# Gated attention, a token mixer and two feed-forward blocks on one core: scores of two block rows in one PSUM pass, full-height blocks in the token mixing, two more heads turned on TensorE

## The chip, the core and the metric

One core of a Trainium2 chip runs one program. Its engines are TensorE (PE, whose weight loads are shown as PEld), VectorE (DVE), ScalarE (ACT), GpSimd (POOL) and SyncE (SP, which here issues every DMA). Each engine works through its own list in order; semaphores join the lists. The metric is the device time of one launch in microseconds, the median of several runs.

## The reference, cut to what matters

```python
# 4 batches x 8 heads, 576 positions, 64 per head: 32 heads in all
scores = (q @ k.T) / 8 + (cum[i] - cum[j])       # cum = cumsum(log f); above the diagonal -1e9
attn = softmax(scores); x = attn @ v             # per head
# token mixing (over the 576 positions), per batch, then channel mixing
h = relu(x.T @ w_tok1) @ w_tok2                  # 576 -> 256 -> 576
u = x + h.T
x2 = u + relu(u @ w_ch1) @ w_ch2                 # 512 -> 1536 -> 512
# second block: 512 -> 1024, a 3-tap convolution over positions as a gate, -> 512
hh = relu(x2 @ w_in); out = (hh * sigmoid(conv(hh))) @ w_out
```

The weights arrive as 64-bit floats and are decoded on the chip.

## The kernel before, in words

**Precision by splitting.** Most products are made from a high and a low part of each operand: `mm3` (lines 231 to 236) issues three matmuls, high by high (L234), high by low (L235), low by high (L236). High parts are written by ACT, low parts by DVE or POOL.

**Attention.** Heads run in pairs. The 576 query rows of a head are cut into five block rows i = 0 to 4 of 64, 128, 128, 128, 128 rows; for causality block row i needs `W[i]` = 64, 192, 320, 448, 576 key columns. `score(p, i)` (lines 666 to 693) makes one block row for both heads of a pair: two matmuls of q by k (L688, one head in array rows 0 to 63, the other in rows 64 to 127) and two that add the decay (`dec`, a row vector spread by `sel`, L692), into a PSUM tile "z". There are two z tiles of two banks each; block row 4 takes both, one a head; any other takes one for both heads. `smax` (L706, DVE) adds the mask and takes the row maximum, `sexp` (L712, ACT) the exponential, into an SBUF tile `t`. A z tile is free again when DVE has read it for both heads.

**Turning the probabilities.** The product with v needs `t` transposed. For heads with `BY_PE` (0 to 7, 30, 31) TensorE turns 13 blocks of 128x128 a head (`ptr`, L745). Heads 0 to 7 are copied out in fp32 (L223, L758); heads 30 and 31 are split into two fp16 halves, the high one by ACT (L763), the low one by DVE (L766). For heads 8 to 29 POOL writes the high half (`hi_part`, L721), DVE the low half (`lo_part`, L727), and two DMA transposes (L737) turn them. Then come the product with v (`pv`, L777 or L782 to L784), and `norm` and `xout` (L789 to L801) on DVE, the split of x by ACT (`xh`) and POOL (`xl`).

**Token mixing.** Four heads make a group, two groups a batch. `t1(g, a)` multiplies x by `w_tok1` over the positions: five blocks, of which block 0 has 64 rows and is contracted with a 64-row matmul, the others 128. `t2(g, d, e)` first turns x into PSUM (`t2_x`, L921: three transposes, of which one is a 64-row or a 32-row one), then adds the second product. From its PSUM tile ACT writes the high part `uh` and a copy `us`; the low part `ul` is written by DVE from PSUM for groups in `SOON` (0, 1, 7), by POOL from the copy for the others.

**Channel mixing and the second block.** Once a batch's u is there, `channel_mix` over the first three of twelve weight blocks is put in as filler between the attention's work; the rest runs after the attention, then the second block. These are long rows of 128x288 matmuls.

**What sets the order.** `Order` collects every task with an engine, a duration, a rank and its dependences, plans them (of the tasks that an engine can start earliest, the lowest rank first; buffers such as the two z tiles and four one-bank "w" tiles count), and then emits the instructions in the planned order. `PER`, the planned time of a head, enters the ranks. The plan is fixed when the program is built: what stands at the head of an engine's list and has to wait holds up all behind it.

Of the kernel before, what the change touches and what calls it, by code (L numbers as in the profile page):

```python
# [9 lines left out]
F32R = mybir.dt.float32r  # L10
# [137 lines left out]
def fox_moe_kernel(  # L148
# [54 lines left out]
    BY_PE = [n < 8 or n >= NH - 2 for n in range(NH)]  # L203

    FULL = 2 * HG
    PER = 7.0
# [12 lines left out]
    def f32(ap):  # L219
        return ap.bitcast(F32)  # L220
# [257 lines left out]
    with tc.manual_schedule():  # L478
# [11 lines left out]
        dec = ap1.tile([128, QKW - S], F32R, name="dec", bufs=1)  # L490
# [39 lines left out]
        nc.scalar.activation(out=dec[:, 0:S], in_=cum, func=AF.Copy, scale=-8.0)  # L530
        for a in (1, 3):
            r = slice(NH * a, NH * a + NH)
            nc.vector.scalar_tensor_tensor(dec[r, 0:S], cum[r], -8.0, f32(dec[r, 0:S]), ALU.mult, ALU.subtract)
        nc.scalar.activation(out=dec[:, S:QKW - S], in_=f32(dec[:, 0:QKW - 2 * S]), func=AF.Copy)
# [59 lines left out]
        def v_pow(g):  # L594
            sc = ap1.tile([128, 2], F32, tag="vsc", name="vsc", bufs=3)
            nc.vector.tensor_scalar(sc[:, 0:1], vps_t[g], 2.0 ** -86, None, ALU.max)
            si = sc[:, 0:1].bitcast(I32)
            nc.vector.tensor_scalar(si, si, 0x7F800000, 0x7F800000, ALU.bitwise_xor, ALU.bitwise_and)
            nc.vector.tensor_scalar(sc[:, 0:1], sc[:, 0:1], 8192.0, None, ALU.mult)
            nc.vector.tensor_scalar(sc[:, 1:2], sc[:, 0:1], PSC * 1e-9, None, ALU.mult)  # L600
            vs_t[g] = sc
# [44 lines left out]
        w1l = ap1.tile([128, NS, TOK], F32R, tag="w1l", name="w1l", bufs=1)  # L646
        w2h = ap1.tile([128, KT, S], F32R, tag="w2h", name="w2h", bufs=1)
# [20 lines left out]
        def score(p, i):  # L668
            t = qk_t[p % QKB]
            w = W[i]  # L670
            rows = 64 if i == 0 else 128
            if i == 4:
                z = [bank("z") for _ in range(2)]
                hw = w // 2
                spans = [(S + 64 + e * hw, hw) for e in range(2)]
                out_ = [[z[x][:, e, 0:hw] for e in range(2)] for x in range(2)]
                for x in range(2):
                    z_t[2 * p + x, i] = z[x][:, :, 0:hw]
            else:
                z = bank("z")  # L680
                spans = [(S, w)]
                out_ = [[z[0:rows, x, 0:w]] for x in range(2)]
                for x in range(2):
                    z_t[2 * p + x, i] = z[0:rows, x, 0:w]
            halves = [slice(64 * x, 64 * x + 64) for x in range(2)]
            for e, (k0, n) in enumerate(spans):
                for x, r in enumerate(halves):
                    nc.tensor.matmul(out_[x][e], t[r, Q0[i]:Q0[i] + rows], t[r, k0:k0 + n], start=True, stop=False)  # L688
            for e, (k0, n) in enumerate(spans):
                for x, r in enumerate(halves):  # L690
                    h = 2 * p + x
                    nc.tensor.matmul(out_[x][e], sel[r, h:h + 1].to_broadcast([64, rows]), dec[r, k0 - S:k0 - S + n],  # L692
                                     start=False, stop=True)
# [127 lines left out]
        PE_S = {4: 1.42, 3: 1.16, 2: 0.89, 1: 0.61, 0: 0.44}  # L821
# [4 lines left out]
        def pair(p):  # L826
# [5 lines left out]
            for i in ORDER:  # L832
                kz = [turn("z") for _ in range(2 if i == 4 else 1)]
                T("PE", PE_S[i], t0 + 1, score, p, i, reads=[kq], writes=[*kz, ("scores",)], pools=A2 + A1, ring=kz)
                for x in range(2):
                    n = 2 * p + x
                    kt = ("t", n % TB)
                    rank = t0 + x * PER
                    T("DVE", DVE_S[i], rank + 2, smax, n, i, reads=[kz[x % len(kz)]], writes=[(*kt, i), ("m", n % 3, i)],
                      pools=A2 + A1, ring=[kz[x % len(kz)]])  # L840
                    T("ACT", ACT_E[i], rank + 3, sexp, n, i, reads=[("m", n % 3, i)], writes=[(*kt, i)], pools=A2)
# [42 lines left out]
        def t1(g, a):  # L884
# [4 lines left out]
            for j in range(NS):  # L889
                r = slice(0, 64 if j == 0 else 128)  # L890
                terms.append((w1h[r, j, c], w1l[r, j, c], st["xh"][r, j, :], st["xl"][r, j, :]))
# [14 lines left out]

        SEGS = [[], []]
        for j in range(NS):
            s0, n = (0, 64) if j == 0 else (64 + 128 * (j - 1), 128)
            for e in range(2):  # L910
                lo, hi = max(s0, e * CH), min(s0 + n, e * CH + CH)
                if lo < hi:
                    SEGS[e].append((j, n, lo - s0, hi - s0, lo - e * CH, hi - e * CH))

        def t2_x(g, d, e):

            st = tok[g]
            ps = bank("w")[:, 0:CH]
            c = slice(d * 128, (d + 1) * 128)
            for k, (j, n, a0, a1, b0, b1) in enumerate(SEGS[e]):  # L920
                nc.tensor.matmul(ps[:, b0:b1], xf_t[g][a0:a1, j, c], ident[a0:a1, a0:a1], is_transpose=True, start=(k == 0),  # L921
                                 stop=False)
            st["ps2", d, e] = ps
# [34 lines left out]
        SOON = (0, 1, NG - 1)  # L958
# [259 lines left out]
```

## Time and profile before

| | us |
|---|---|
| median of 3 runs | 781.96 |
| lowest, highest | 779.5, 787.52 |
| the profiled execution | 782.84 |
| its span, first to last instruction | 781.0 |
| TensorE busy | 762.8 (98%) |
| VectorE busy | 491.5 (63%) |
| GpSimd busy | 364.7 (47%) |
| ScalarE busy | 338.7 (43%) |

Attention, token mixing and the filler take the first 290 us; the rest is channel mixing and the second block. A busy time counts an instruction from its start to its modelled end; matmuls overlap, so what a matmul costs TensorE is read from one start to the next, not from its duration. A pair's start is below that of its first score matmul with 288 columns (block row 4): pair 4 (heads 8 and 9) starts at 76.85 us, pair 5 at 107.12, pair 11 (heads 22 and 23) at 198.31.

### The profile page before, as it was taken

Reading aid. Unit: us, or ns where it says so; the run is one execution under the profiler, and the core shown is the slowest. Engines: PE = TensorE matmul, PEld = TensorE weight load, DVE = VectorE, ACT = ScalarE, POOL = GpSimd, SP = SyncE. Lnnn points to the kernel's source line nnn. Section 1 sums busy time; section 2 is a strip of 40 time slices with the busy share of each in tenths; the row PEclk is TensorE's granted clock in tenths of the full one; section 3 lists DMA queues with packets and bytes.
Section 4 is the critical chain, followed back from the end, with each engine's and each line's share of the span. In section 5 each row is a group of like instructions: output and inputs, shape, how many; then the busy total and the mean of one; then the engine's idle time right before and its main releaser. Section 6 shows DMA issues by size and latency. Waiting matters only on the chain.

```text
span 781.0 us, 16260 instructions
## 1 busy us (share of the span) xinstructions
PE 762.8 (98%) x6428; PEld 714.1 (91%) x6428; DVE 491.5 (63%) x1075; ACT 338.7 (43%) x753; POOL 364.7 (47%) x448
## 2 busy tenths in 40 slices
PE   7999899999999999999999999999998999999997
PEld 5888788888888899999999999999998999999997
DVE  5687869777695667688731221124799866787651
ACT  5676545566465555653320220122453333233321
POOL 3253635784757335454521221223666655565441
PEclk6899889999999999999999999999999999999999
DMA  9344489899997906755442122124421110100000
GB/s 222 102 159 151 153 168 194 170 220 204 199 183 156 188 2 213 266 192 162 129 138 75 39 70 84 31 69 146 161 77 47 53 55 31 54 20 20 31 33 31
DMA packets 133453, 91.69 MB, mean 117 GB/s; under 512 B 86848, under 2 KB 125504, under 8 KB 133376
## 3 DMA queue, kind: packets, MB, share of 16 engines
q1 hardware_dynamic: 133376, 90.65, 45.1%
q8 instruction: 50, 0.82, 0.4%
q14 instruction: 27, 0.22, 0.1%
HBM read 53.01 MB, written 18.87 MB: 92 GB/s over the span
## 4 chain that ended last, share of the span: by engine, by line
PE 84%; DVE 10%; DMA 2%; ACT 1%; issue 1%; POOL 1%; SPq 0%; POOLq 0%; ACTq 0%; DVEq 0%
PE w L234 14%; PE w L235 13%; PE w L236 13%; PE z L235 8%; PE z L234 8%; PE z L236 8%; PE z L688 7%; PE w L777 3%; DVE cv L1119 3%; PE w L921 2%; PE z L692 2%; PE w L745 2%; DVE wexp L307 1%; PE w L782 1%; PE w L783 1%; PE w L784 1%
## 5 line engine op out<-in xcount | busy, mean ns | idle before, releaser
L234 PE MATMUL w<-uh,ww2a 128*128 128x288 f32 x352 | 104.3, 296 | 0.6 <-DVE r L425 0.5
L235 PE MATMUL w<-ul,ww2a 128*128 128x288 f32 x352 | 103.8, 295 | 0.0
L236 PE MATMUL w<-uh,ww2a 128*128 128x288 f32 x352 | 103.6, 294 | 0.0
L421 ACT ACTIVATE r<-w 128x288 fp32r<-128x288 f32 x96 | 39.0, 408 | 132.0 <-PE w L236 131.2
L712 ACT ACTIVATE t<-t,m 128x320 f32<-128x320 f32 (+4 forms) x160 | 82.5, 554 | 30.0 <-DVE m L706 27.1
L1119 DVE SCALAR_TENSOR_TENSOR cv<-hp,cw,cv 128x286 f32<-128x286 f32 (+1 forms) x128 | 89.1, 696 | 4.5
L234 PE MATMUL w<-uh,ww 128*128 128x288 f32 x288 | 86.8, 301 | 0.5 <-ACT hp L1112 0.5
L425 DVE SCALAR_TENSOR_TENSOR r<-w,r 128x288 fp32r<-128x288 f32 x96 | 42.9, 454 | 70.3 <-ACT r L421 70.0
L234 PE MATMUL z<-r,ww2b 128*128 128x288 f32 x288 | 85.0, 295 | 0.0
L235 PE MATMUL w<-ul,ww 128*128 128x288 f32 x288 | 85.0, 295 | 0.0
L706 DVE CUSTOM_DVE_ANT_0 t<-z,mask 128x320 f32<-128x320 f32 (+4 forms) x160 | 71.6, 482 | 21.3 <-PE z L692 20.6
L235 PE MATMUL z<-r,ww2b 128*128 128x288 f32 x288 | 84.8, 295 | 0.0
L236 PE MATMUL w<-uh,ww 128*128 128x288 f32 x288 | 84.7, 294 | 0.0
L236 PE MATMUL z<-r,ww2b 128*128 128x288 f32 x288 | 84.7, 294 | 0.0
L229 POOL TENSOR_TENSOR ul<-u,uh 128x288 fp32r<-128x288 f32 x64 | 57.9, 930 | 54.5 <-ACT uh L223 54.5
L234 PE MATMUL z<-g,ww2a 128*128 128x286 f32 (+1 forms) x256 | 76.1, 297 | 2.2 <-ACT o L223 1.0
L235 PE MATMUL z<-g,ww2a 128*128 128x286 f32 (+1 forms) x256 | 76.3, 298 | 1.6 <-POOL g L229 1.6
L236 PE MATMUL z<-g,ww2a 128*128 128x286 f32 (+1 forms) x256 | 75.4, 295 | 0.0
L688 PE MATMUL z<-qk 64*128 64x288 f32 (+4 forms) x384 | 67.6, 441 | 7.8 <-DVE m L706 5.6
L442 POOL TENSOR_TENSOR res<-res,u 128x288 f32<-128x288 f32 x32 | 26.2, 820 | 93.1 <-DVE res L439 85.9
L234 PEld LDWEIGHTS w<-uh,ww2a 128*128 128x128 f32 x352 | 66.0, 187 | 1.0 <-DVE r L425 1.0
L236 PEld LDWEIGHTS w<-uh,ww2a 128*128 128x128 f32 x352 | 66.3, 188 | 0.0
(136 smaller groups left out, 2187.4 us busy)
## 6 DMA issues: line engine op xcount, KB each, us to landing
wraw<-in_moe_w_ch_dram SPq DMA_DIRECT2D x24, 512.0 KB, 4.0
qk<-in_qk_dram SPq DMA_DIRECT2D x16, 608.0 KB, 4.4
u_d<-us SPq DMA_DIRECT2D x8, 576.0 KB, 4.4
p_d<-res SPq DMA_DIRECT2D x32, 144.0 KB, 3.1
u<-u_d SPq DMA_DIRECT2D x8, 576.0 KB, 5.0
res<-p_d SPq DMA_DIRECT2D x32, 144.0 KB, 2.6
x_d<-res SPq DMA_DIRECT2D x32, 144.0 KB, 1.8
u<-x_d SPq DMA_DIRECT2D x8, 576.0 KB, 4.1
```

The source lines that it names most:

```text
L229: nc.gpsimd.tensor_tensor(o, a, b, ALU.subtract)
L234: nc.tensor.matmul(ps, wh, xh, start=(first and i == 0), stop=False)
L235: nc.tensor.matmul(ps, wh, xl, start=False, stop=False)
L236: nc.tensor.matmul(ps, wl, xh, start=False, stop=(last and i == n - 1))
L421: nc.scalar.activation(out=t[:, 0, :], in_=box["z", m], func=AF.Relu)
L425: nc.vector.scalar_tensor_tensor(t[:, 1, :], box["z", m], 0.0, f32(t[:, 0, :]), ALU.max, ALU.subtract)
L442: nc.gpsimd.tensor_tensor(box["res", d], box["res", d], ubox["u"][:, d], ALU.add)
L688: nc.tensor.matmul(out_[x][e], t[r, Q0[i]:Q0[i] + rows], t[r, k0:k0 + n], start=True, stop=False)
L706: nc.vector.tensor_tensor_reduce(to, z_t.pop((n, i)), mk, -0.125, 3e38, ALU.add, ALU.min, m_t[n][0:rows, i:i + 1])
L712: nc.scalar.activation(out=tt[0:rows, o:o + w], in_=tt[0:rows, o:o + w], func=AF.Exp, bias=m_t[n][0:rows, i:i + 1], scale=-1.0)
L777: nc.tensor.matmul(o[:, 0:65], p32(n)[:, 128 * blk:128 * blk + 128], vp32_t[g][:, slot, hh, :], start=(j == 0), stop=(j == nb - 1))
L1119: nc.vector.scalar_tensor_tensor(cv, hp[:, s0 + t:s1 + t], cw[:, t, m:m + 1], cv, ALU.mult, ALU.add)
```

## The change

Block rows 0 and 3 now share one z bank a head (64 + 448 = 512 columns), and so do 1 and 2 (192 + 320); the decay of both is added by one matmul of 512 columns, for which `dec` holds the needed pieces side by side. A 64-row block 0 is made with all 128 rows (the lower 64 are not read). In `t1` block 0 is contracted over 128 rows, the lower 64 of its weights being zero; in `t2_x` the transposes that straddle a chunk are made whole, and only the 64-row one is left. Heads 8 and 9 are turned by TensorE. The low part of u of groups 2 and 3 (the second batch) is written by DVE. `PER` goes from 7 to 6, and the planner's score durations follow the new blocks.

```diff
-    BY_PE = [n < 8 or n >= NH - 2 for n in range(NH)]
+    BY_PE = [n < 10 or n >= NH - 2 for n in range(NH)]
-    PER = 7.0
+    PER = 6.0
...
+        DEC4, DEC12 = 128, S + 128
+        dec = ap1.tile([128, DEC12 + 512], F32R, name="dec", bufs=1)
+        dmain = dec[:, 64:64 + S]
...
-        nc.scalar.activation(out=dec[:, S:QKW - S], in_=f32(dec[:, 0:QKW - 2 * S]), func=AF.Copy)
+        for a, n in ((DEC12 - 64, 64), (0, 64), (DEC12, W[1]), (DEC12 + W[1], W[2])):
+            nc.scalar.activation(out=dec[:, a:a + n], in_=f32(dmain[:, 0:n]), func=AF.Copy)
...
+        nc.gpsimd.memset(f32(w1h[64:128, 0]), 0.0)
+        nc.gpsimd.memset(f32(w1l[64:128, 0]), 0.0)
...
+        SETS = {(4,): DEC4, (0, 3): 0, (1, 2): DEC12}
-        def score(p, i):
+        def score(p, blocks):
...
+                z = bank("z")
+                sums = [([z[:, x, :] for x in range(2)], d0, 512)]
+                products = []
+                at = 0
+                for i in blocks:
+                    products.append((i, [z[:, x, at:at + W[i]] for x in range(2)], S, W[i], at == 0))
...
+            for i, out_, k0, n, first in products:
                 for x, r in enumerate(halves):
-                    nc.tensor.matmul(out_[x][e], t[r, Q0[i]:Q0[i] + rows], t[r, k0:k0 + n], start=True, stop=False)
+                    nc.tensor.matmul(out_[x], t[r, Q0[i]:Q0[i] + 128], t[r, k0:k0 + n], start=first, stop=False)
...
-        PE_S = {4: 1.42, 3: 1.16, 2: 0.89, 1: 0.61, 0: 0.44}
+        PE_S = {(4,): 1.42, (0, 3): 1.33, (1, 2): 1.28}
...
-                r = slice(0, 64 if j == 0 else 128)
-                terms.append((w1h[r, j, c], w1l[r, j, c], st["xh"][r, j, :], st["xl"][r, j, :]))
+                terms.append((w1h[:, j, c], w1l[:, j, c], st["xh"][:, j, :], st["xl"][:, j, :]))
...
-            for k, (j, n, a0, a1, b0, b1) in enumerate(SEGS[e]):
-                nc.tensor.matmul(ps[:, b0:b1], xf_t[g][a0:a1, j, c], ident[a0:a1, a0:a1], is_transpose=True, start=(k == 0),
-                                 stop=False)
+            for k, (j, b) in enumerate(SEGS[e]):
+                n = 64 if j == 0 else 128
+                nc.tensor.matmul(ps[:, m + b:m + b + n], xf_t[g][0:n, j, c], ident[0:n, 0:n], is_transpose=True,
+                                 start=(k == 0), stop=False)
...
-        SOON = (0, 1, NG - 1)
+        SOON = (0, 1, 2, 3, NG - 1)
```

The order is planned anew. TensorE's list before, from the product with v of heads 6 and 7 (`vp`, `pt`) to the token mixing of group 1 (`xh`, `w1h`); between them stand block rows 3, 2, 1, 0 of pair 4:

```order
L777 MATMUL w<-vp_149,pt 128x65 x30
L688 MATMUL z<-qk_105 128x448 x2
L692 MATMUL z<-dec,sel 128x448 x2
L688 MATMUL z<-qk_105 128x320 x2
L692 MATMUL z<-dec,sel 128x320 x2
L688 MATMUL z<-qk_105 128x192 x2
L692 MATMUL z<-dec,sel 128x192 x2
L688 MATMUL z<-qk_105 64x64 x2
```

The same place in the changed program (`ident,t` are the transposes of heads 8 and 9, the 288-column scores are block row 4 of pair 5):

```order
L704 MATMUL z<-dec,sel 128x512 x2
L789 MATMUL w<-vp_152,pt 128x65 x15
L700 MATMUL z<-qk_105 128x192 x2
L700 MATMUL z<-qk_105 128x320 x2
L704 MATMUL z<-dec,sel 128x512 x2
L757 MATMUL w<-ident,t_139 128x128 x8
L757 MATMUL w<-ident,t_140 128x128 x8
L595 MATMUL w<-vacc,ones 128x1
L700 MATMUL z<-qk_106 128x288 x4
L704 MATMUL z<-dec,sel 128x288 x4
L234 MATMUL w<-xh,w1h 128x256
```

The scores now stand on both sides of head 7's product with v, and 16 transposes and pair 5's first scores stand between that product and the token mixing of its group.

VectorE's list before at this place: `rs` and `xf` are norm and xout of heads 6 and 7, the `wexp` triples decode weights, the last row reads the first score tile of block row 3:

```order
L801 TENSOR_TENSOR xf<-w,rs 128x5x64
L305 TENSOR_SCALAR wexp<-wexp 128x512
L306 SCALAR_TENSOR_TENSOR wexp<-wraw,wexp 128x512
L307 SCALAR_TENSOR_TENSOR wexp<-wraw,wexp 128x512
L789 TENSOR_SCALAR rs<-w 128x5
L793 RECIPROCAL rs<-rs 128x5
L305 TENSOR_SCALAR wexp<-wexp 128x512
L306 SCALAR_TENSOR_TENSOR wexp<-wraw,wexp 128x512
L307 SCALAR_TENSOR_TENSOR wexp<-wraw,wexp 128x512
L801 TENSOR_TENSOR xf<-w,rs 128x5x64
L706 ISA t_136,m<-z,mask 128x448
```

And in the changed program, from the norm of head 6 to the xout of head 7:

```order
L805 RECIPROCAL rs<-rs 128x5
L718 ISA t_139,m<-z,mask 128x448
L718 ISA m 128x1
L813 TENSOR_TENSOR xf<-w,rs 128x5x64
L718 ISA t_139,m<-z,mask 64x64
L718 ISA m 64x1
L718 ISA t_140,m<-z,mask 128x448
L718 ISA m 128x1
L801 TENSOR_SCALAR rs<-w 128x5
L805 RECIPROCAL rs<-rs 128x5
L718 ISA t_140,m<-z,mask 64x64
L718 ISA m 64x1
```

No weight is decoded between the two heads any more; the two decodes stand ahead of head 6's norm instead.

## Rows read from the trace of the kernel before

**Rows 1.** The page: busy time, share, instructions; TensorE's clock in 40 slices.

```profile
PE   762.8 (98%) x6428; PEld 714.1 (91%) x6428; DVE 491.5 (63%) x1075; ACT 338.7 (43%) x753; POOL 364.7 (47%) x448
```

**Rows 2.** Busy time by stretch, then granted clock, DMA share, GB/s.

```profile
76.85:107.12 30.27, 26.89 (x177) 23.22 (x177) 23.00 (x52) 15.89 (x35) 16.54 (x19) 0.83 0.54 145
107.12:198.31 91.19, 90.26 (x1036) 75.72 (x1035) 69.44 (x200) 55.02 (x119) 53.78 (x53) 1.00 0.95 196
...
120.00:140.00 20.00, 19.14 (x226) 15.99 (x222) 17.79 (x53) 11.96 (x24) 11.19 (x13) 1.00 1.13 203
```

**Rows 3.** TensorE's timeline at pair 4: start, us, line, idle before and its releaser.

```profile
88.02 0.55 PE L692 MATMUL z<-dec,sel 64*128 64x320 f32 x2
91.07 0.60 PE L688 MATMUL z<-qk 64*128 64x192 f32 x4 [2.50 <-DVE m L706]
...
92.03 0.36 PE L234 MATMUL w<-xh,w1h 64*128 64x256 f32 x1
93.27 0.58 PE L235 MATMUL w<-xl,w1h 64*128 64x256 f32 x1 [0.89 <-POOL xl L229]
```

**Rows 4.** TensorE's timeline: scores that stand alone, then two block rows in one run.

```profile
169.07 1.02 PE L688 MATMUL z<-qk 64*128 64x448 f32 x4
...
170.22 0.40 PE L234 MATMUL w<-r,ww 128*128 128x288 f32 x1
...
170.82 0.81 PE L688 MATMUL z<-qk 64*128 64x320 f32 x4
...
171.71 0.40 PE L234 MATMUL w<-r,ww 128*128 128x288 f32 x1
...
189.06 1.02 PE L688 MATMUL z<-qk 64*128 64x448 f32 x4
...
190.90 0.40 PE L234 MATMUL w<-uh,ww 128*128 128x288 f32 x1
```

**Rows 5.** The same view: block rows 1 and 0 in one run.

```profile
146.21 0.59 PE L688 MATMUL z<-qk 64*128 64x192 f32 x4
...
147.26 0.40 PE L234 MATMUL w<-uh,ww 128*128 128x288 f32 x1
```

**Rows 6.** The same view: token mixing across its 64-row block.

```profile
142.43 0.28 PE L236 MATMUL w<-xh,w1l 128*128 128x256 f32 x1
142.64 0.38 PE L234 MATMUL w<-xh,w1h 64*128 64x256 f32 x1
...
143.41 0.28 PE L235 MATMUL w<-xl,w1h 128*128 128x256 f32 x1
143.53 0.28 PE L236 MATMUL w<-xh,w1l 128*128 128x256 f32 x1
```

**Rows 7.** The same view: `t2_x` with its 32-row transpose; 16 transposes of `ptr`.

```profile
105.56 0.29 PE L236 MATMUL w<-w2h,t1l 128*128 128x288 f32 x1
105.78 0.62 PE L921 MATMUL w<-ident,xf 32*128 32x32 f32 x3
106.15 0.38 PE L234 MATMUL w<-w2h,t1h 128*128 128x288 f32 x1
...
35.19 1.97 PE L745 MATMUL w<-ident,t 128*128 128x128 f32 x16
```

**Rows 8.** VectorE by line and shape, 57.84 to 260.85 us: count | busy us, mean ns.

```profile
L727 DVE SCALAR_TENSOR_TENSOR pl<-t,ph 128x1024 f16<-128x1024 f32 x21 | 28.8, 1373 | 1.2 <-POOL ph L721 1.0
L727 DVE SCALAR_TENSOR_TENSOR pl<-t,ph 128x640 f16<-128x640 f32 x21 | 23.3, 1115 | 4.9 <-POOL ph L721 4.9
...
L948 DVE TENSOR_TENSOR ul<-w,uh 128x288 fp32r<-128x288 f32 x8 | 3.7, 456 | 3.9 <-ACT us L223 3.8
```

**Rows 9.** The same view, 270 to 290 us: the low half of heads 30 and 31.

```profile
L766 DVE SCALAR_TENSOR_TENSOR pt<-w,pt 128x512 f16<-128x512 f32 x6 | 3.9, 685 | 0.1
```

## What the change will do to the time: the prediction

> **What bounds the kernel now.** I read the page's busy times first, then busy time by stretch, then TensorE's timeline at single places, then VectorE by line and shape. The page has TensorE busy 98% of the span [rows 1]; no other engine is near. That share is counted to modelled ends, so I took what a matmul costs from the distance between starts: two 256-column matmuls in a row start 0.12 us apart (143.41 to 143.53 [rows 6]), so by columns 288 take 0.135. From 290 us on the program is almost nothing but rows of 288, and the change does not touch them. So what it can change lies in the first 290 us, where TensorE pays for its own work and for what it waits for.
>
> The largest wait is at pair 4. The score matmuls that start at 88.02 are followed by the next at 91.07, where TensorE waited 2.50 us for VectorE to empty a z tile; at 92.03 one matmul of the token mixing starts and its neighbour only at 93.27, after 0.89 us for GpSimd's `xl` [rows 3]. Against the usual spacing these are 2.6 and 1.0 us. And the clock falls: over the 30.27 us from pair 4 to pair 5 the granted clock is 0.83 [rows 2], which with the two levels of 1.2 and 2.4 GHz is a third of the stretch, 10.3 us, at the lower one. Work of about 5 us took 10. The whole place costs 2.6 + 1.0 + 5 = 8.6 us. What came before the fall were these two waits; in the 20 us of [rows 2] with the clock at 1.00 TensorE was kept busy.
>
> **The change, part by part.** *Scores.* Block row 3 alone takes 170.22 - 169.07 = 1.15 us for 448 columns, block row 2 takes 171.71 - 170.82 = 0.89 for 320; both in one run take 190.90 - 189.06 = 1.84 [rows 4]. So a run has a fixed part of about 0.20 us, and the rest goes by columns. A run also costs its neighbours: the three 288-column matmuls between two runs, 170.22 to 170.82, take 0.60 us where 3 x 0.135 is 0.40. That makes 0.40 us a run. The column total of a pair is the same before and now (1600 a head). What goes is runs: in the two lists of TensorE I counted 58 and 38 runs of scores, 20 x 0.40 = 8.0 us. Block row 0 also no longer changes the array's tile inside a run: rows 1 and 0 together take 147.26 - 146.21 = 1.05 us for 256 columns [rows 5], where the fixed 0.20 and 2.1 ns a column (1.64 / 768) make 0.74. That 0.3 us stands in the 8 pairs that have rows 1 and 0 in one run: 2.4. Together **-10.4 us**. Nothing gained would need a 512-column pass to cost as much as two runs, which the 1.84 excludes; by the run counts alone it is 8.0.
>
> *Token mixing.* From 142.43 to 143.41 five spacings take 0.98 us with block 0 in them; at 0.12 each they would take 0.60 [rows 6]. 0.38 us a `t1`, 16 of them: **-6.1 us**. Zeroing the lower weight halves is two short GpSimd fills at the start, beside the first loads.
>
> The Trainium skill, "TensorE: Matmul & The Clock Gate" under "LDWEIGHTS (loading the stationary operand)", says that a load takes its time from columns and that 32 rows take as long as 128. By that alone 64 rows made into 128 save nothing, and this term would be 0 and the time 774. The 0.98 against 0.60 of [rows 6] is not in it: there the neighbours of the 64-row block are slowed. "TensorEngine Tiling (Array Packing)", Key Properties, says that a change of tiling mode drains the engine, and the trace agrees with that.
>
> *Transposes of the token mixing.* A chunk with the 32-row transpose takes 106.15 - 105.56 = 0.59 us from the matmul before to the matmul behind [rows 7]; three whole ones at 0.12 after a spacing of 0.135 take 0.48 to 0.50. At 0.48, 16 of them: **-1.8 us**. The 96 to 128 widening of the other chunk is at most 0.01 each by the same 0.12.
>
> *Heads 8 and 9.* 26 more transposes at 1.97 / 16 = 0.12 [rows 7]: **+3.1 us** of TensorE. Four DMA transposes, four GpSimd passes and four VectorE passes go. ScalarE and VectorE take the split, in eight pieces each. TensorE's own work thus shrinks by 10.4 + 6.1 + 1.8 - 3.1 = **15.2 us**.
>
> *The place at pair 4.* Before, two weight decodes stand on VectorE between the norms and the first read of block row 3, so z stays full. In the new list the decodes stand ahead of head 6's norm, the reads of the first tile lie between the two norms, and TensorE has 16 transposes and pair 5's first scores (16 x 0.12 plus 576 columns, 3.3 us together) between head 7's product and its group's token mixing. I expect both waits gone and with them the fall of the clock: **-8.6 us**. Bounds: 0 if they come back elsewhere, -8.6 if nothing takes their place.
>
> *What comes in their place.* Less time for TensorE leaves less for VectorE. From pair 4 to pair 11 it is busy 23.00 + 69.44 = 92.4 of 30.27 + 91.19 = 121.5 us, 76%, with 252 instructions [rows 2]. Between the two pairs' first reads of a z tile its list holds 245 before and 267 now. For the 245 I take 92.4 less 7 at the mean of 0.37, 90. The 22 more are: 8 `ul` of the second batch (8 x 0.456 = 3.6 [rows 8]); 8 low-half pieces of heads 8 and 9 (six at 0.65 and two small ones, 4.7 [rows 9]); two `lo_part` pieces less (1.37 + 1.12 = 2.5 [rows 8]); and eight others at the mean, 3. That is 8.8, with the overlap of neighbours 8: **98 us**. TensorE's own work there is the 121.5 less 8.6 at pair 4, less 60 filler matmuls that the plan moves out (8.0), less eight runs (3.2) and six token mixings with their transposes (3.0), plus the 3.1 of heads 8 and 9, less about 1 of small waits: **101 us**. So VectorE would have to be busy 97% for TensorE never to wait. It hardly can: its reads of z, its norms and its `t1l` each stand in line until a matmul has ended. The best 20 us of before have it at 17.79 / 20 = 89% [rows 2]. At 89% the stretch takes 110 us, 9 more than TensorE's own. I take **+9 us**; the bounds are 0 (97%) and 98 / 0.76 - 101 = +28 (the share of before). The `ul` on VectorE cost 3.6 of this; on GpSimd, busy 70.3 of the 121.5 us, they were hidden.
>
> *DMA.* The mean share of the DMA engines is 0.95 from pair 5 to pair 11, and 1.13 in 20 us of it [rows 2], so 0.95 is not the end of what they do. There are four transposes fewer, and the stretch is some 10% shorter, which cancels. I price it at 0; what it could cost is within (b).
>
> Sum: -15.2 - 8.6 + 9 = -14.8, against the profiled execution's 782.84: **768 us**. The median of the runs is 781.96, 0.9 below that execution.
>
> **The rivals.** (a) *VectorE keeps up.* No new waits: -23.8, 759 us. For it: much of its idle time is waiting for TensorE, and that shrinks when it is behind. Against: 97% has no example in the rows.
>
> (b) *The long wait and the low clock come elsewhere.* The 8.6 us stay, and the first 30 us, or the new rows of transposes, hold another: 768 + 8.6 = 777. For it: VectorE is nearly full from pair 4 on, and one wait of 2.5 us was enough before. Against: in 120 to 140 us VectorE is at 89% and the clock at 1.00 [rows 2]. The Trainium skill's "TensorE: Matmul & The Clock Gate", Part 4, has it that transposes do not count as activity for the full clock, which would put the fall at the new transposes of heads 8 and 9. In this trace 16 transposes in a row take 0.12 us each [rows 7], which is no halved speed.
>
> (c) *VectorE sets the pace, slower than before.* If it holds only its 76%, pairs 4 to 11 take 129 us instead of 121.5: -15.2 - 8.6 + 28 = +4.2, 787 us. The change breaks even where the new waits reach 23.8 us, a share of 98 / 125 = 78%. For it: the list is in order, and a block of z now waits for four reads instead of two. Against: the 76% holds pair 4's stalled TensorE and its slow clock, and 89% was held for 20 us [rows 2].
>
> (d) *The height of a block does not matter.* The 0.38 us around a 64-row block is a wait for something else, and token mixing and its transposes give nothing: 768 + 6.1 + 1.8 = 776. Against: the spacings around the block are the same wherever they are not held up by a semaphore, as in [rows 6], where nothing is marked as waited for. The rule on columns of "TensorE: Matmul & The Clock Gate" in the Trainium skill would have it so.
>
> **How the numbers follow.** Forecast (763 to 774) 0.53; (a) 0.13; (b) 0.17; (c) 0.10; (d) 0.07. The range runs from 757, just under (a), to 780, just over (b) and (d): it leaves out (c) and the outer edges, under 0.2. Faster by over 1% (about what a measurement of this kernel can tell from no change) is below 774: 0.53 less a little, (a), and a few of (b) and (d), 0.68. Within 1%: the rest of (b), (d) and part of (c), 0.25. Slower: the far part of (c), 0.07.
>
> **What would show it.** Right: a score run of two block rows takes about 1.3 us from its first matmul to the next; `t1` starts stand 0.12 apart throughout; no 2 us gap on TensorE and a clock of 1.00 between 75 and 110 us; pair 11 starts near 185 us instead of 198; VectorE above 85% from pair 4 to pair 11; rows of waits of TensorE for `m` L718 that add up to some 9 us. Wrong: pair 11 near 190 us or later, a second stretch at 1.2 GHz behind the start, or more waits of TensorE for VectorE or for the DMA transposes of heads 12 and 15, whose time between two products with v the new list shortens. The stages from 290 us on should keep their length; if they grow, the terms above cannot say why.

## The result: 770.7 us, 1.5% less than before

| | before | changed |
|---|---|---|
| median, us | 782.3 | 770.7 |
| lowest, highest | 779.5, 787.5 | 769.5, 774.9 |
| the profiled execution | 782.84 | 771.39 |
| its span | 781.0 | 769.2 |

The ratio is 0.9854, 95% interval 0.9822 to 0.9887. The forecast was 768.0 with a range of 757 to 780.

The page of the changed kernel, busy time by engine, beside [rows 1]: TensorE is still busy 97% of a shorter span.

```profile
PE 749.2 (97%) x6390; PEld 710.4 (92%) x6390; DVE 491.7 (64%) x1087; ACT 341.2 (44%) x764; POOL 353.4 (46%) x438
```

Changed kernel, busy time by stretch (from, to, length; TensorE, weight loads, VectorE, ScalarE, GpSimd; granted clock, DMA share, GB/s), to be read beside [rows 2]: the start, pairs 4 to 11, the place of the old stall, two new places, and the stages behind the attention.

```profile
0.00:18.40 18.40, 14.04 (x67) 10.50 (x67) 9.91 (x32) 9.99 (x19) 5.62 (x30) 0.81 0.95 210
71.14:182.96 111.82, 106.96 (x1152) 91.73 (x1152) 89.27 (x262) 70.19 (x154) 58.19 (x63) 0.95 0.78 170
75.00:110.00 35.00, 34.04 (x340) 30.02 (x341) 30.12 (x86) 24.05 (x54) 16.54 (x20) 1.00 0.62 161
116.24:132.98 16.74, 14.52 (x156) 12.03 (x156) 11.82 (x41) 8.87 (x17) 10.70 (x12) 0.80 0.72 147
147.02:160.55 13.53, 12.26 (x108) 9.64 (x107) 10.33 (x35) 7.79 (x16) 9.58 (x11) 0.87 1.04 174
319.90:769.20 449.30, 441.59 (x3301) 439.50 (x3300) 252.72 (x436) 140.44 (x321) 196.26 (x237) 1.00 0.25 76
```

The old stall is gone: from 75 to 110 us the clock is 1.00. Pairs 4 to 11 take 111.82 us, before 121.46. But the clock is at 0.80 and 0.87 in two stretches that ran at 1.00 before. The part behind the attention, from the first matmul with the weight tile `ww2a` on, keeps its length: 449.3 us, before 450.0 (331.0 to 781.0).

What happened at 116 us: TensorE's timeline of the changed kernel (start, length, line, shape, idle time before it and its releaser).

```profile
116.24 0.75 PE L700 MATMUL z<-qk 64*128 64x288 f32 x2
119.21 1.33 PE L700 MATMUL z<-qk 64*128 64x288 f32 x4 [2.22 <-DVE m L718]
...
147.02 0.75 PE L700 MATMUL z<-qk 64*128 64x288 f32 x2
149.04 1.21 PE L700 MATMUL z<-qk 64*128 64x288 f32 x4 [1.27 <-DVE vsc L600]
```

And VectorE's list at the first of them, the same view:

```profile
115.07 0.28 DVE L804 TENSOR_SCALAR rs<-w,vsc 128x5 f32<-128x5 f32 x1 [0.57 <-PE w L796]
115.39 0.19 DVE L805 RECIPROCAL rs<-rs 128x5 f32<-128x5 f32 x1
115.49 1.30 DVE L739 SCALAR_TENSOR_TENSOR pl<-t,ph 128x1024 f16<-128x1024 f32 x1
116.79 0.46 DVE L425 SCALAR_TENSOR_TENSOR r<-w,r 128x288 fp32r<-128x288 f32 x1
117.17 0.48 DVE L813 TENSOR_TENSOR xf<-w,rs 128x320 f32<-128x320 f32 x1
117.56 0.81 DVE L739 SCALAR_TENSOR_TENSOR pl<-t,ph 128x640 f16<-128x640 f32 x1
118.30 0.48 DVE L718 CUSTOM_DVE_ANT_0 t<-z,mask 128x320 f32<-128x320 f32 x1
...
118.71 0.35 DVE L718 CUSTOM_DVE_ANT_0 t<-z,mask 128x192 f32<-128x192 f32 x1
```

TensorE has issued the first score matmul of pair 7's block row 4 (one head's first 288 columns) and needs the other z tile, which waits for the reads of block rows 2 and 1 of the second head of the pair before (118.30 and 118.71). These were ready, but stand behind a norm that itself waited for a product of TensorE, two low-half passes, an `r` pass of the filler (L425) and an `xout`: 3.2 us of other work from 115.07 to 118.30. It is the mechanism of the old place at pair 4, 28 us later; at 147 us it comes again with one read behind a norm, a low-half pass and an `xout` (the row names `vsc`, a one-column instruction that VectorE runs right behind that read).

### The profile page after: what moved, and what is told of

It reads as the page before. It is cut to its first block, busy times and chain, and to the rows that moved or that the text cites. A ratio compares the mean times of both kernels' runs of the same rounds, so it can differ in the third digit from the quotient of the medians.

```text
span 769.2 us, 16204 instructions
## 1 busy us (share of the span) xinstructions
PE 749.2 (97%) x6390; PEld 710.4 (92%) x6390; DVE 491.7 (64%) x1087; ACT 341.2 (44%) x764; POOL 353.4 (46%) x438
## 4 chain that ended last, share of the span: by engine, by line
PE 84%; DVE 10%; ACT 2%; DMA 2%; issue 1%; POOL 1%; SPq 0%; POOLq 0%; ACTq 0%; DVEq 0%
PE w L234 13%; PE w L236 13%; PE w L235 13%; PE z L235 9%; PE z L234 9%; PE z L236 9%; PE z L700 7%; PE w L789 4%; DVE cv L1134 3%; PE z L704 2%; PE w L757 1%; DMA wraw<-in_moe_w_ch_dram 1%; PE w L794 1%; PE w L795 1%; PE w L796 1%; DVE pl L739 1%
## 5 line engine op out<-in xcount | busy, mean ns | idle before, releaser
L724 ACT ACTIVATE t<-t,m 128x448 f32<-128x448 f32 (+4 forms) x160 | 81.1, 554 | 15.4 <-DVE m L718 15.0
L425 DVE SCALAR_TENSOR_TENSOR r<-w,r 128x288 fp32r<-128x288 f32 x96 | 42.5, 454 | 66.6 <-ACT r L421 66.3
L718 DVE CUSTOM_DVE_ANT_0 t<-z,mask 64x64 f32<-64x64 f32 (+4 forms) x160 | 70.1, 480 | 17.3 <-PE z L704 17.0
L700 PE MATMUL z<-qk 64*128 64x288 f32 (+4 forms) x384 | 63.5, 436 | 8.3 <-DVE m L718 5.4
L236 PEld LDWEIGHTS w<-uh,ww2a 128*128 128x128 f32 x352 | 66.3, 188 | 0.0
L235 PEld LDWEIGHTS w<-ul,ww2a 128*128 128x128 f32 x352 | 66.1, 188 | 0.0
```

Of the source, the lines that this page charges most:

```text
L235: nc.tensor.matmul(ps, wh, xl, start=False, stop=False)
L236: nc.tensor.matmul(ps, wl, xh, start=False, stop=(last and i == n - 1))
L425: nc.vector.scalar_tensor_tensor(t[:, 1, :], box["z", m], 0.0, f32(t[:, 0, :]), ALU.max, ALU.subtract)
L700: nc.tensor.matmul(out_[x], t[r, Q0[i]:Q0[i] + 128], t[r, k0:k0 + n], start=first, stop=False)
L718: nc.vector.tensor_tensor_reduce(to, z_t.pop((n, i)), mk, -0.125, 3e38, ALU.add, ALU.min, m_t[n][0:rows, i:i + 1])
L724: nc.scalar.activation(out=tt[0:rows, o:o + w], in_=tt[0:rows, o:o + w], func=AF.Exp, bias=m_t[n][0:rows, i:i + 1], scale=-1.0)
```

## The experiments

All ratios are to the kernel before, in the same runs. To compare an experiment with the changed kernel, take its ratio beside 0.9854 (0.9822 to 0.9887). Every edit of a rank, a buffer count or a list makes the plan anew, unless the text says that the order stays.

### 1. Token mixing alone, in the kernel before

```diff
-                r = slice(0, 64 if j == 0 else 128)
-                terms.append((w1h[r, j, c], w1l[r, j, c], st["xh"][r, j, :], st["xl"][r, j, :]))
+                terms.append((w1h[:, j, c], w1l[:, j, c], st["xh"][:, j, :], st["xl"][:, j, :]))
```

with the zeroed weight halves and the whole transposes of `t2_x`.

> The kernel before, with nothing changed but the token mixing: block 0 of t1 is contracted over 128 rows and the straddling transposes of t2_x are whole. Every engine's list keeps its order. Forecast: 6.1 us from t1 and 1.8 us from the transposes, all of it on TensorE's own path, so 782.3 - 7.9 = 774.4, a ratio to the kernel before of 0.990. Rival (d), the height of a block does not matter: 782.3, a ratio of 1.000. Between the two: the work shrinks but part of it turns into waits; then the t1 starts stand 0.12 us apart in its trace and the stall at pair 4 (2.5 us for m, 0.9 us for xl) is longer than before.

Measured: 776.6 us, ratio 0.9919 (0.9890 to 0.9949), that is 6.3 us less (4.0 to 8.6; by the two medians, 781.3 and 776.6, it is 4.7). Its TensorE timeline across block 0, beside [rows 6]:

```profile
137.27 0.28 PE L234 MATMUL w<-xh,w1h 128*128 128x256 f32 x1
137.38 0.28 PE L235 MATMUL w<-xl,w1h 128*128 128x256 f32 x1
137.50 0.28 PE L236 MATMUL w<-xh,w1l 128*128 128x256 f32 x1
137.62 0.28 PE L234 MATMUL w<-xh,w1h 128*128 128x256 f32 x1
```

The starts stand 0.12 us apart. The height of the block does cost its neighbours time; rival (d) is out. The order being the same, waits can only follow from the shorter work, and some do: TensorE waits 2.1 us for an `r` pass (L425) of VectorE at 299 us; before, its waits for `r` added up to 0.5. The two waits at pair 4 are 2.50 and 0.77 us, much as before (2.50 and 0.89), but the clock from 85 to 110 us is 0.93 where it was 0.80.

### 2. Scores alone, in the kernel before

The `SETS` and `dec` part of the change and the planner's durations for it, nothing else.

> The kernel before with the scores side by side and nothing else of the change (PER 7, heads 8 and 9 turned by DMA, token mixing with 64-row blocks, low u of groups 2 and 3 on GpSimd). Forecast of the scores' term: -10.4 us; counted again from the runs in the trace of the changed kernel, about -8. If the stall at pair 4 stays as it is: 782.3 - 8 to 10.4 = 772 to 774. If the new order also removes it: 8.6 less, 763 to 766. Rival: the work that TensorE saves comes back as waits for VectorE, which now frees a z tile only after four reads: 780 or more.

Measured: 779.3 us, ratio 0.9959 (0.9934 to 0.9983): 3.2 us less (1.3 to 5.2), where the work saved is about 8 (worked out from the runs of scores, below). The stall at pair 4 is still there and longer than in [rows 3], the clock beside it lower than the 0.83 of [rows 2]. Timeline and stretch of this kernel:

```profile
88.92 2.29 PE L696 MATMUL z<-qk 64*128 64x64 f32 x8 [2.87 <-DVE m L714]
```

```profile
85.00:110.00 25.00, 22.13 (x192) 18.49 (x193) 19.51 (x49) 11.69 (x26) 15.67 (x19) 0.73 0.64 155
```

A second loss stands behind the attention. Its waits of TensorE from 320 to 400 us (in total, times, longest):

```profile
PE z L234 <- DVE res L439: 3.2, 3, 1.5
PE z L236 <- POOL ww2b L229: 0.8, 1, 0.8
```

Before and in the changed kernel this stretch has no wait above 0.5 us. `res` (L439) is VectorE's read of a z tile; in its list these reads stand behind passes that decode weights. `ww2b` is decoded weights. Experiments 4 and 5 look further.

### 3. Parts of the changed kernel taken back, one at a time

```diff
-    PER = 6.0
+    PER = 7.0
```

```diff
-    BY_PE = [n < 10 or n >= NH - 2 for n in range(NH)]
+    BY_PE = [n < 8 or n >= NH - 2 for n in range(NH)]
```

```diff
-        SOON = (0, 1, 2, 3, NG - 1)
+        SOON = (0, 1, NG - 1)
```

> The changed kernel with PER back at 7 and nothing else changed: the plan then puts more of the filler matmuls into the attention, which ends later. Theory: the decode of the 18 weight blocks of the channel mixing can only begin when the attention's memory is free; in the changed kernel its first high part is written at 272.3 us, its last low part at 342.0, 69.7 us later, and TensorE reads that group of blocks first at 343.9, so there is no slack. With PER at 7 the decode begins at 280 or later (280.9 in the kernel with only the scores changed, 284.4 in the kernel before) and ends at 350 or later; TensorE, whose own work is the same, waits some 6 us for weights between 335 and 385 us: 776 to 779. Rival: PER only reorders work that TensorE has to do anyway: 770.7 within 2 us.

> The changed kernel with heads 8 and 9 turned by DMA transposes again. By the terms of the forecast: 3.1 us less for TensorE, some 2 us less for VectorE (4.7 of low-half pieces against 2.5 of low-half passes), so 765.5 to 767.6. Rival: the transposes of heads 8 and 9 were the cover in which pair 4's reads and the split of x are done; without them the stall and the half clock at pair 4 come back, 8.6 us less the 3 to 5: 774 to 776.

> The changed kernel with the low part of u of groups 2 and 3 back on GpSimd: 8 passes of 0.456 us fewer on VectorE, 3.6 us. If VectorE's sum of work sets the pace between pair 4 and pair 11: 770.7 - 3.6 = 767.1. If the places in its list do: whatever the new order gives at pairs 7 and 9; if the reads of z still stand behind the low-half passes there, 770.7 within 2 us, and if the waits go by chance of the new order, down to 762.

| | median, us | ratio |
|---|---|---|
| PER back at 7 | 768.4 | 0.9833 (0.9813 to 0.9854) |
| heads 8 and 9 by DMA | 770.1 | 0.9850 (0.9830 to 0.9870) |
| low u of groups 2, 3 on GpSimd | 768.1 | 0.9816 (0.9784 to 0.9848) |

None of the three is worth anything by itself that these runs can tell. `PER` does not move the end of the attention: the decode behind it begins at 272.2 us with 7 and at 272.3 with 6, so my theory for that run was wrong. Without heads 8 and 9 on TensorE the saved 3.1 us go into a new wait in pair 5 (1.74 us for `t1l`, clock 0.93 over 26 us). With 3.6 us taken from VectorE, the wait at 119 us stays at 2.2 us and the one at 149 goes, while one of 0.9 us comes at 180; 2.5 us by the medians does not tell the two theories apart. Behind that same wait of 2.2 us the clock is 0.89 over pair 7 (15.51 us), in the changed kernel 0.80 (16.74 us).

### 4. The reads first

Both heads' reads of a z tile get the rank of the first head's, in the changed kernel and in the kernel before.

```diff
-                    T("DVE", DVE_S[i], rank + 2, smax, n, i, reads=[kz[x % len(kz)]], writes=[(*kt, i), ("m", n % 3, i)],
+                    T("DVE", DVE_S[i], t0 + 2, smax, n, i, reads=[kz[x % len(kz)]], writes=[(*kt, i), ("m", n % 3, i)],
```

> The changed kernel with one edit in the planner: the reads of the z tiles (smax) of the second head of a pair get the rank of the first head's, 6 lower than now, so that they no longer stand behind the first head's low-half passes and the norm of the head before. VectorE's work is the same, only its order differs. Theory that places in VectorE's list make the loss: the waits at 116.6 to 119.2 us and 147.4 to 149.0 us go and the two stretches at half clock behind them (6.8 and 3.4 us) with them; these two places cost 5.8 + 3.5 us in the trace of the changed kernel, so 770.7 - 9.3 = 761.4, a ratio to the changed kernel of 0.988, and to the kernel before of 0.973. Rival, that VectorE's sum of work sets the pace: the waits only move, pairs 4 to 11 take 111.8 us as now, and the time stays within 2 us of 770.7.

Measured in the changed kernel: 768.6 us, ratio 0.9818 (0.9789 to 0.9847). Its pairs 4 to 11, then its waits of TensorE from 320 to 400 us:

```profile
64.05:176.95 112.90, 111.88 (x1200) 97.56 (x1199) 97.66 (x270) 74.70 (x165) 68.31 (x69) 1.00 0.84 192
```

```profile
PE z L234 <- DVE res L439: 2.5, 3, 1.4
PE z L234 <- ACT ww2b L223: 2.3, 2, 1.5
PE z L236 <- POOL ww2b L229: 2.1, 2, 1.3
PE z L235 <- DVE r L425: 0.5, 1, 0.5
```

The theory of places holds in the attention: the clock is 1.00, TensorE is busy 111.88 of 112.90 us and does 48 matmuls more than the changed kernel in such a stretch. VectorE is busy 86% of it, so the 80% of the changed kernel was no ceiling. The stretch itself is no shorter (112.90 us, before 111.82), as the rival had it; the gain is in the matmuls that it holds. But the end came only 2 us earlier (the two intervals overlap), because 7.4 us of waits came back behind the attention, with the clock at 0.98 over these 80 us: 4.4 for decoded weights (`ww2b`), 2.5 for reads of z tiles behind decode passes (`res`), 0.5 for an `r` pass.

> The kernel before with the one edit of the kernel with the reads first: both heads' reads of the z tiles get the first head's rank. It prices the place at pair 4 by itself. Forecast's term: the waits of 2.5 and 0.9 us and the 10.2 us at half clock go, 8.6 us: 781.4 - 8.6 = 772.8. Rival, that the decode of weights behind the attention is a second bound: if its first high part is still written near 284 us, TensorE gives the gain back as waits for weights between 345 and 390 us: 779 to 782.

Measured in the kernel before: 787.3 us, ratio 1.0063 (1.0044 to 1.0082), slower. At pair 5 TensorE waits only 1.05 us now, and the clock falls all the same:

```profile
86.86:113.51 26.65, 26.41 (x216) 22.19 (x216) 18.19 (x50) 11.49 (x27) 14.31 (x14) 0.75 0.70 177
```

There are 63 runs of scores in its list instead of 58, and 4.8 us of waits between 320 and 400 us. Taking the wait away did not bring the 8.6 us.

### 5. The decode of weights behind the attention

When the attention's memory is free, 18 weight blocks of the channel mixing are loaded and decoded (ScalarE, VectorE, ScalarE, GpSimd in turn) while TensorE still does other work. By tile (count, shortest/median/longest ns, first to last start): ScalarE's first high part of `ww2a`, GpSimd's last low part of `ww2b`, TensorE's first matmul with it. These are starts; a last low part takes 1.3 to 1.8 us more. The changed kernel:

```profile
L223 ACT ACTIVATE ww2a<-wexp x9: 617/632/642, 272.3 to 300.8; 128x512 fp32r<-128x512 f32 x9
```

```profile
L229 POOL TENSOR_TENSOR ww2b<-wexp,ww2b x9: 1284/1299/1774, 312.2 to 342.0; 128x512 fp32r<-128x512 f32 x9
```

```profile
L234 PE MATMUL z<-r,ww2b x77: 293/295/402, 343.9 to 399.9; 128*128 128x288 f32 x77
```

The kernel with the reads first:

```profile
L229 POOL TENSOR_TENSOR ww2b<-wexp,ww2b x9: 1268/1295/1736, 306.7 to 338.4; 128x512 fp32r<-128x512 f32 x9
```

```profile
L234 PE MATMUL z<-r,ww2b x86: 292/295/442, 331.0 to 399.6; 128*128 128x288 f32 x86
```

In the changed kernel the last low part starts 1.9 us ahead of the first matmul with this group; before it was 1.2 us (353.5 and 354.7), so there it ended behind that matmul. No wait came of it, since TensorE takes the nine blocks in turn, three matmuls of 0.13 us each, and needs the last some 3 us after the first. With the reads first TensorE comes 12.9 us earlier to a decode whose last low part starts 3.6 us earlier. Three runs ask what holds the decode.

First a third buffer for the decoded weights:

```diff
-            box["t"] = work.tile([128, WSTN], F32, tag="wexp", name="wexp", bufs=2)[0:p, 0:n]
+            box["t"] = work.tile([128, WSTN], F32, tag="wexp", name="wexp", bufs=3)[0:p, 0:n]
```

> The kernel with the reads first (768.6 us), with three buffers for the decoded weights instead of two, so that ScalarE can begin a block while VectorE and GpSimd still have the two before. In that kernel TensorE waited between 335 and 372 us for decoded weights, nine gaps that are 8.6 us longer than usual, with 3.4 us at half clock. Theory: the decode is held up by the hand-over of two buffers (VectorE waited 14.1 us for ScalarE's first step between 280 and 380 us), so a third takes most of these waits away: 768.6 - 6 to 10 = 759 to 763. Rival: VectorE's own work sets the pace of the decode (85% busy from 320 to 360 us): at most 2 us, 767 or more.

Measured: 769.4 us, ratio 0.9846 (0.9828 to 0.9864). The waits for weights are gone (the last low part starts at 335.6 instead of 338.4), but nothing is gained: the new plan waits elsewhere, 3.3 us for `m` (2.7 with two buffers) and 1.7 for `ul` among them.

Then the reads-first kernel with one decode pass left out:

```diff
-            nc.vector.scalar_tensor_tensor(c, box["raw"][0:p, 0:n, 1], -2 ** 31, c, ALU.bitwise_and, ALU.bitwise_or)
+            if n != 512 or key[0] not in ("ch1", "ch2") or key[1] < M1:
+                nc.vector.scalar_tensor_tensor(c, box["raw"][0:p, 0:n, 1], -2 ** 31, c, ALU.bitwise_and, ALU.bitwise_or)
```

> The kernel with the reads first (768.6 us), in which the second of the three decode passes of VectorE (L306, the sign) is left out for the 18 weight blocks of the channel mixing that are decoded behind the attention: 0.69 us a block less for VectorE, 12.4 in all, in the same order; the values are wrong in sign. If VectorE's work sets the pace of the decode, it ends some 10 us earlier and the waits between 335 and 372 us go: 758 to 761. If loads and hand-overs set it, a block still takes nearly as long: 766 or more.

Measured: 767.6 us, ratio 0.9815 (0.9791 to 0.9838). The last low part starts at 336.2 instead of 338.4, though VectorE has 12.4 us less to do. From the first high part on that is 65.5 us instead of 68.7, so VectorE's passes are at most a small part of what holds the decode. Waits of 1.9 us for `ww2b` and 3.9 for `res` are left.

And a third buffer for the weights as loaded:

```diff
-            box["raw"] = work.tile([128, WSTN, 2], I32, tag="wraw", name="wraw", bufs=2)
+            box["raw"] = work.tile([128, WSTN, 2], I32, tag="wraw", name="wraw", bufs=3)
```

> The kernel with the reads first (768.6 us) with three buffers for the weights as loaded (wraw) instead of two; decoded weights (wexp) keep two. Theory: a load of 512 KB takes 3.7 us to land and can only be issued when VectorE has finished with one of two buffers (SyncE waited 37.3 us for L307 of VectorE between 265 and 345 us), so the 18 blocks of the channel mixing take 68.7 us (269.7 to 338.4) whatever TensorE does, and TensorE, which came 13 us earlier to them, waited there. With a third buffer the decode ends at 330 or earlier, the nine gaps of together 8.6 us and the 3.4 us at half clock between 335 and 372 us go: 758 to 762. Rival: VectorE's work (three passes a block and the rest of the channel mixing) sets the pace: the decode ends at 337 or later, 767 or more.

Measured: 764.9 us, ratio 0.9781 (0.9755 to 0.9807), the fastest of all.

```profile
L229 POOL TENSOR_TENSOR ww2b<-wexp,ww2b x9: 1283/1470/1821, 298.5 to 328.5; 128x512 fp32r<-128x512 f32 x9
```

```profile
L234 PE MATMUL z<-r,ww2b x91: 288/295/348, 334.6 to 400.0; 128*128 128x288 f32 x91
```

The last low part starts 9.9 us earlier than with two buffers and TensorE waits for no weight. Some 3 of these come from an attention that ends earlier in the new plan (266.5 instead of 269.7 us at the first high part); the 18 blocks take 62.0 us instead of 68.7, so the two load buffers held the decode more than VectorE's pass did. The gain, 3.7 us by the medians, is less than the 6 to 10 expected: the new plan has other waits, 4.2 us for `r` passes and 1.8 us for one `xl`.

> The changed kernel, with its own order of reads, and three buffers for the loaded weights: the other half of the kernel with both edits (764.9 us). Theory of two bounds close together: in the changed kernel TensorE reaches the second group of weight blocks at 343.9 us, 1.9 us after the last of them is decoded, so TensorE's own lateness (the places at 116 and 147 us) is what the end waits for, and a faster decode alone gives at most 2 us: 769 to 771. Rival: the third buffer alone is what made the kernel with both edits faster: 765 to 767.

Measured: 770.9 us, ratio 0.9861 (0.9841 to 0.9881): as the changed kernel. So the reads first alone give 2 us, which these runs hardly tell from nothing, the third buffer alone nothing, both 6. That fits two bounds that lie close together, but does not show them. This run is not a clean half: its plan also lost the long waits at 116 and 147 us and got others (1.7 and 1.4 us for `r` passes at 307 and 361 us). And TensorE's lateness is not what held its end: it comes to `ww2b` at 339.0 us, 4.9 us earlier than in the changed kernel, and takes 429.8 us from there to the end instead of 425.3. The wait at 361 us is 1.4 of these 4.5; most of the rest is a lower clock in the last 20 us, here and then in the changed kernel:

```profile
750.00:768.80 18.80, 13.51 (x83) 12.50 (x81) 1.19 (x3) 2.10 (x5) 2.53 (x4) 0.87 0.10 32
```

```profile
750.00:769.20 19.20, 14.17 (x99) 13.16 (x97) 3.16 (x7) 2.96 (x7) 2.52 (x4) 1.00 0.09 32
```

### 6. A smaller pace

> The kernel with the reads first (768.6 us) with PER at 5 instead of 6: filler matmuls go behind the attention, which ends earlier, and the decode of weights with it. Theory that the attention's end decides: its decode begins before 265 us instead of 269.7, the waits for weights between 335 and 372 us (8.6 us and the half clock) shrink by as much as it begins earlier, 760 to 764. Rival: the attention already goes as fast as VectorE lets it, so that fillers taken out of it leave TensorE waiting there instead: m L718 gains what the weights lose, 768.6 or more.

Measured: 768.7 us, ratio 0.9835 (0.9808 to 0.9863). The decode begins at 266.8 instead of 269.7, and TensorE waits for no weights, but 2.5 us for `r` passes and 1.2 us for `xh` have come. So it is the rival in its time, though not by the wait for `m` that it named (1.9 us, with `PER` at 6 2.7).

## Why the prediction was right, and where its steps were not

The time lay in the forecast case (763 to 774). Term by term, for the profiled executions:

| term | forecast | found | from |
|---|---|---|---|
| scores | -10.4 | -8.3 | worked out from the runs below |
| token mixing and its transposes | -7.9 | -6.3 (-8.6 to -4.0) | experiment 1 |
| heads 8 and 9 | +3.1 | (+3.1) | not measured apart |
| place at pair 4 | -8.6 | -7.8 | one wait of 0.85 us left there |
| new waits, pairs 4 to 11 | +9 | +10.5 | stretches above |
| clock at the start | none | -5.1 | below |
| waits for `m` behind pair 11 | none | +1.6 | 0.67 and 0.88 us at 188 and 204 us |
| sum | -14.8 | -12.3 | measured: -11.5 |

*Scores.* Right in kind, the size off. The changed kernel's runs of two block rows, with the matmul that follows each:

```profile
109.38 1.25 PE L700 MATMUL z<-qk 64*128 64x64 f32 x8
...
110.79 0.40 PE L234 MATMUL w<-uh,ww 128*128 128x288 f32 x1
...
112.18 1.13 PE L700 MATMUL z<-qk 64*128 64x192 f32 x8
...
113.48 0.20 PE L794 MATMUL w<-vp,pt 128*128 128x65 f16 x1
```

Rows 1 and 2 take the 1.30 us that was forecast, rows 0 and 3 take 1.41: 0.13 above what the fixed part and 512 columns make (1.28), in 16 pairs 2.1 us. A run with block row 0 in it, though made whole, costs 0.11 more than one without. That gives -8.3. In the kernel with only this edit it brought 3.2 us; a longer stall at pair 4 and the waits behind the attention stand against the rest.

*Token mixing.* The mechanism held, and so did the sum of its two parts; 0.12 us from start to start was seen. But each part was mis-sized, and the errors cancel, which is luck. Two `t1` stand in one run of 30 matmuls, and the 0.38 us was read at the second. The run as a whole, from its first matmul to the one behind it, before and then in the kernel of experiment 1:

```profile
207.78 0.36 PE L234 MATMUL w<-xh,w1h 64*128 64x256 f32 x1
...
212.00 0.20 PE L782 MATMUL w<-vp,pt 128*128 128x65 f16 x1
```

```profile
202.98 0.39 PE L234 MATMUL w<-xh,w1h 128*128 128x256 f32 x1
...
206.68 0.20 PE L784 MATMUL w<-vp,pt 128*128 128x65 f16 x1
```

That is 4.22 against 3.70 us; eight such runs give 4.2 us, not 6.1. The transposes, in the kernel of experiment 1, beside [rows 7]:

```profile
59.72 0.30 PE L236 MATMUL w<-w2h,t1l 128*128 128x288 f32 x1
59.86 0.49 PE L924 MATMUL w<-ident,xf 128*128 128x128 f32 x3
60.10 0.38 PE L234 MATMUL w<-w2h,t1h 128*128 128x288 f32 x1
```

They take 0.38 us where 0.48 was forecast, against 0.59 before: 16 times 0.21 is 3.4 us, not 1.8. Together 7.6 us, within the interval of experiment 1.

The rule of "TensorE: Matmul & The Clock Gate" in the Trainium skill, under "LDWEIGHTS (loading the stationary operand)", that a load takes its time from columns and not from rows, would have had the change in experiment 1 give nothing; 0.9949 is the upper end of its interval, so the measurement decides against reading it that way.

*The place at pair 4.* In the changed kernel both waits and the slow clock are gone, as forecast. As a term of its own it did not hold: in the kernel before, the reads-first edit cut the wait from 2.5 to 1.05 us and the clock fell still. Nor is the clock's part a fixed price of the two waits: with much the same waits it was 0.80 from 85 to 110 us in the kernel before and 0.93 in experiment 1, a lower level for 10 and for 3.5 us. What was priced as one wait and its consequence is a property of the whole list there.

*New waits.* This step had the right size for the wrong reason. I took VectorE to be full: 98 us of work at a share of 89%. In the changed kernel it worked 89.3 us in 111.8, 80%: the work itself was put 9 us too high, and the waits for `m` add up to 2.6 us there (5.4 in the whole span), not 9. The loss came at two places, where reads of z stand behind other work and the clock falls behind the wait: 2.6 + 1.7 us longer than usual between two starts, and 6.7 + 3.5 us at the lower clock (0.4 of 16.74 and 0.26 of 13.53 us), half of which is lost, 5.1: 9.4 together, with 1.1 in two smaller waits. That was rival (b), the long wait coming elsewhere, and I had given it 777 because I added it to a full VectorE. The reads-first kernel, with VectorE at 86% and TensorE waiting 1 us, shows that no full VectorE stood behind it.

*The start* was in no term. At the clock of 0.81 over 18.40 us some 7.0 us ran at the lower level, before 14.5 (0.67 over 21.95); half the difference is 3.7 us. Before, the lower level ran on behind that point (0.83 over the next 8.05 us, 2.7 us), which costs 1.4 more. The token mixing alone, whose list begins as before, has 0.80 over its first 21.13 us, so this is more an execution's chance than the change's: up to 5.1 of the 11.5 us between the two profiled executions are luck.

*What would show it.* Pair 11 starts at 182.96 (185 was said), the clock is 1.00 from 75 to 110, no wait for DMA transposes came, and the stages behind kept their length. VectorE above 85% and 9 us of waits for `m` were wrong; a second stretch at the lower clock, which was to speak against the forecast, came twice.

*What the forecast did not see* is that the decode ran hardly ahead of TensorE already: its last low part started 1.2 us before the group's first matmul. The terms could add up because the changed plan freed the attention's memory 12.1 us earlier (272.3 against 284.4 us at the first high part), about as much as TensorE gained up to its first matmul with `ww2b` (343.9 against 354.7). Token mixing alone, in the same order, brings that from 284.4 to 277.7, the scores alone to 280.9, so most of it is the attention's own work that got shorter; the rest was not settled, and `PER`, 7 or 6, is not the cause. With the scores alone, where TensorE came to `ww2b` 8.7 us earlier and that memory was free only 3.5 us earlier, part of the gain came back as waits.

## What to carry to other kernels

Read how far each supply (here decoded weights) runs ahead of the engine that sets the time, not only how long that engine waits for it: a supply that is a few us ahead shows no wait and can still be the next bound. In lists that are in order, price a late buffer by what stands ahead of its reader, not by the sum of that engine's work. When single edits each give next to nothing, try them together: here the reads first and the third load buffer did, for a reason that these runs fit but do not prove. A single profiled execution carries some us of clock that another of the same list does not; compare stages before comparing spans.

## What was not expected of the hardware

What brings the clock down stays open. It fell behind waits of 1.05 to 2.9 us at the places above, but not behind this one, in the kernel with both edits, whose next 19 us ran at 1.00:

```profile
51.32 0.39 PE L235 MATMUL w<-xl,w1h 128*128 128x256 f32 x1 [1.79 <-POOL xl L229]
```

```profile
51.00:70.00 19.00, 18.68 (x153) 17.09 (x153) 14.36 (x38) 13.16 (x29) 8.65 (x10) 1.00 0.47 152
```

And at the end of the program the same three waits for `g` (0.6, 0.6 and 0.5 us) stand in the changed kernel, whose clock stays at 1.00, and in the one with the third buffer alone, where it is 0.87 over the last 18.8 us (experiment 5). The length of a wait alone does not tell whether the clock will fall.
